# Summing exp tiles ahead of the row-sum products, and FFN1 of the last tiles by seven block products, in a fused attention and FFN kernel

## The chip, the cores and the metric

The kernel runs on one core of one Trainium2 chip. The metric is device time in microseconds (us) of one execution, lower is better, given as the median of several executions.

Engines: PE is TensorE (matrix products), PEld its weight loads, DVE is VectorE, ACT is ScalarE, POOL is GpSimd, which also issues most loads. The program lists the steps of all engines in one order, and each engine gets its instructions in that order.

## The reference

Eight batches of attention with eight heads, 576 queries, 16 beacon keys that all queries see and 576 causal keys, then an FFN with ELU over all 4,608 tokens (shortened).

```python
def _attn_ref(q, k, v, beacon_k, beacon_v):        # B, H, S, D = 8, 8, 576, 64; Nb = 16
    k_all = np.concatenate([beacon_k, k], axis=2)
    v_all = np.concatenate([beacon_v, v], axis=2)
    scores = scale * np.matmul(q, k_all.transpose(0, 1, 3, 2))
    scores = np.where(causal, -1000000000.0, scores)       # beacon keys are never masked
    scores = scores - scores.max(-1, keepdims=True)
    a = np.exp(scores)
    a /= a.sum(-1, keepdims=True) + 1e-09
    return np.matmul(a, v_all)

def _moe_ref(x, w_in, w_out):                      # x: 4608 x 512, w_in: 512 x 2048
    h = x @ w_in
    g = np.where(h > 0.0, h, np.exp(np.minimum(h, 0.0)) - 1.0)
    return g @ w_out
```

## The kernel before

The program is a list of short words, each one step: `S` scores, `x` exp (ACT), `m` causal mask (DVE), `L` row sums, `n` their reciprocals (ACT), `W` exp times values, `M` the scaling into the FFN input (DVE), `F` one row block of FFN1, `e u k` (or `e r g`) ELU (ACT and DVE), `Q` products of FFN2. FFN2 already works by seven block products from tile 2 on (a Winograd scheme: `Z` are its operand sums, `J` its copies and additions out of PSUM). `warm` and `wm` are filler: products of zeros that nobody reads. A round of the body holds the FFN1 of tile b, the FFN2 of tile b-1 and the attention of batches b and b+1. Rounds 3 to 7 have attention; what follows, with tile 8 and the last FFN2, is the tail.

```python
    def quad(b, g, qa, qe, t, half, first):          # row sums (half None) or value sums
        v16 = vt[b]
        pcs = [(j, max(a, qa), min(e, qe), c + max(a, qa) - a) for (j, a, e, c) in lays[b]
               if max(a, qa) < min(e, qe)]
        for n, (j, a, e, c) in enumerate(pcs):       # 5 key chunks, in pieces
            for i in range(4):                       # 4 heads, one 32-column group each
                h, p = 4 * g + i, 2 * g + i // 2
                nc.tensor.matmul(
                    out=t[32 * i:32 * (i + 1), a - qa:e - qa],
                    lhsT=ones[0:kc[j], :] if half is None else v16[0:kc[j], j, h, 32 * half:32 * (half + 1)],
                    rhs=ets[b, p][0:kc[j], i % 2, c:c + e - a],
                    start=(first and n == 0), stop=(n == len(pcs) - 1), skip_group_check=True)
    # ...
    def quads(b, g, half, name):
        t = psum.tile([P, 1024], FP32, tag="S", name=name)[:, 512 - QA:512 - QA + S]
        quad(b, g, 0, QA, t[:, 0:QA], half, True)    # QA = 112
        quad(b, g, QA, S, t[:, QA:S], half, True)
        return t
    # ...
    def F(t, i):                                     # FFN1: 4 products of 512 columns
        # ...
        for n_ in range(512 // w):
            fc = i * (512 // w) + n_
            for cc in range(NCC):
                nc.tensor.matmul(
                    out=h[:, n_, :], lhsT=w_in16[:, cc, P * fc:P * (fc + 1)],
                    rhs=xt[k][:, cc, a - TT * k:e - TT * k], start=(cc == 0), stop=(cc == NCC - 1))
    # ...
    def load_wi(c):                                  # c = 0..3, 512 columns each
        f_ = slice(512 * c, 512 * (c + 1))
        for g in range(2):
            for t in range(2):
                nc.gpsimd.dma_start(out=w_in16[:, 2 * g + t, f_], in_=wi_v[:, :, g, t, f_])
    # ...
    def cb(b, p):                                    # 16 beacon keys, once for each pair of heads
        qkT[b, p] = qks[p]
        nc.vector.tensor_copy(out=qkT[b, p][:, 1, 0:NB], in_=bkT[:, p, NB * b:NB * (b + 1)])
    # ...
    def r(t, i):                                     # one form of the ELU, used up to tile 2
        nc.vector.tensor_scalar(
            out=rb[t, i], in0=eb[t, i], scalar1=1.0, scalar2=1.0, op0=ALU.min, op1=ALU.subtract)
    # ...
    BODY = """
    F.b.0 e.b.0 u.b.0 k.b.0 Q.z.0.7 Z.z.1.1 S.b.1.0 x.b.1.0 m.b.1.0 S.b.1.1 x.b.1.1 m.b.1.1
    F.b.1 e.b.1 u.b.1 k.b.1 Q.z.7.14 S.b.1.2 x.b.1.2 m.b.1.2 S.b.1.3 x.b.1.3 m.b.1.3 lt.c F.b.2
    e.b.2 u.b.2 k.b.2 Q.z.14.21 J.z.0 Z.z.2.0 L.b.0 W.b.0.0 n.b.0 M.b.0.0 F.b.3 e.b.3 u.b.3
    ...
    """
```

A piece `S.b.1.0` takes two PSUM banks of a tag with two such pairs, shared by scores, row sums and value sums.

The softmax here doesn't subtract the row's maximum and nothing guards it: scores larger than these inputs give would overflow.

## Time and profile before

| | before |
|---|---|
| time, median of the first 3 runs | 352.89 us |
| span of the profiled execution | 349.8 us |
| PE busy | 335.8 us, 96%, 3,651 products |
| DVE busy | 242.3 us, 69%, 514 instructions |
| ACT busy | 281.2 us, 80% |
| POOL busy | 91.7 us, 26% |
| first FFN1 product | at 24.5 us |
| first FFN2 block product (call it Q) | at 105.7 us |
| last product ends | at 346.0 us |

From the page's slices of the kernel before, the row of DVE (busy tenths in 40 equal slices):

```profile
DVE  2672689689798758675867676767776767667661
```

DVE is at 6 to 7 tenths from the middle on: this is the room that the change wants to use.

### The profile page before, as it was taken

The page shows a single profiled execution, that of the slowest core. Times are in us where ns is not written, and L with a number is a line of the kernel's source. Part 1 is how long each engine was busy: PE and PEld are TensorE (multiplying, and loading weights), DVE is VectorE, ACT ScalarE, POOL GpSimd, SP SyncE. Part 2 cuts the span into 40 slices and gives each one's busy share as a digit, 9 for nine tenths or more (in the row PEclk, how much of TensorE's full clock was granted, in tenths as well). Part 3 has the DMA queues.
Part 4 walks back from the last instruction along what each step waited for, and adds up shares of the span by engine and source line. Part 5 has one row for each costly group of instructions (what it writes and reads, how often), then busy time and mean ns, then how long its engine had stood idle before and what let it go on. Part 6 is the DMA issues. An engine that isn't in the chain of part 4 may idle for free.

```text
span 349.8 us, 8839 instructions
## 1 busy us (share of the span) xinstructions
PE 335.8 (96%) x3651; PEld 204.6 (59%) x3651; DVE 242.3 (69%) x514; ACT 281.2 (80%) x473; POOL 91.7 (26%) x120
## 2 busy tenths in 40 slices
PE   8887998989999999999999999999999999999995
PEld 3454655444455656656665666565665666666684
DVE  2672689689798758675867676767776767667661
ACT  1893998679868997999799979997999676777731
POOL 8877446493009107300640050000000000000000
PEclk9998999999999999999999999999999999999999
DMA  9999999999709998993799359300100010010022
GB/s 117 147 150 141 185 182 174 155 140 154 136 33 152 138 114 79 175 137 73 74 172 154 66 63 182 84 2 32 62 32 2 32 60 32 30 63 30 32 90 91
DMA packets 136232, 34.67 MB, mean 99 GB/s; under 512 B 119040, under 2 KB 135680, under 8 KB 136192
## 3 DMA queue, kind: packets, MB, share of 16 engines
q0 software_dynamic: 102080, 18.51, 67.7%
q1 hardware_dynamic: 33536, 15.47, 20.1%
q8 instruction: 28, 0.46, 0.5%
q10 hardware_dynamic: 576, 0.13, 0.2%
q14 instruction: 12, 0.10, 0.1%
HBM read 37.22 MB, written 15.34 MB: 150 GB/s over the span
## 4 chain that ended last, share of the span: by engine, by line
PE 81%; ACT 5%; DMA 4%; DVE 4%; POOL 3%; issue 1%; DVEq 0%; ACTq 0%; POOLq 0%
PE hps L432 34%; PE ops L542 28%; PE ut L322 6%; PE sc L285 6%; DMA w_in<-in_moe_w_in_dram 4%; PE lt L322 3%; PE ops L478 3%; ACT et L295 2%; ACT e L442 1%; DVE qk L259 1%; POOL kst L134 1%; POOL qst L134 1%; DVE r L464 1%; ACT r L447 1%; POOL v L147 1%
## 5 line engine op out<-in xcount | busy, mean ns | idle before, releaser
L432 PE MATMUL hps<-xT,w_in 128*128 128x512 f16 (+1 forms) x640 | 148.9, 359 | 3.9 <-DMA w_in<-in_moe_w_in_dram 2.5
L457 DVE SCALAR_TENSOR_TENSOR gt<-e,r 128x512 f16<-128x512 f32 x133 | 92.0, 692 | 59.2 <-ACT r L447 54.3
L442 ACT ACTIVATE e<-hps 128x512 f32<-128x512 f32 x144 | 89.3, 621 | 33.7 <-PE hps L432 32.6
L295 ACT ACTIVATE et<-sc 128x832 f16<-128x832 f32 x128 | 106.0, 897 | 2.7 <-PE sc L285 2.6
L542 PEld LDWEIGHTS <-gt 128*128 128x128 f16 x768 | 75.1, 98 | 29.0 <-issue 0.3
L447 ACT ACTIVATE r<-hps 128x512 f16<-128x512 f32 x133 | 82.8, 624 | 5.0 <-PE hps L432 2.5
L432 PEld LDWEIGHTS <-w_in 128*128 128x128 f16 x640 | 56.5, 98 | 50.0 <-issue 7.4
L542 PE MATMUL ops<-wt,gt 128*128 128x256 f16 x384 | 52.5, 273 | 0.0
L542 PE MATMUL ops<-w_out,gt 128*128 128x256 f16 x384 | 51.4, 273 | 0.0
L311 DVE TENSOR_TENSOR et<-et,triu 128x256 f16<-128x256 f16 (+2 forms) x164 | 41.8, 357 | 13.2 <-ACT et L295 11.0
L147 POOL DMA_DIRECT2D v<-in_v_dram x40 | 35.5, 977 | 5.7 <-DMA w_out<-in_moe_w_out_dram 1.7
L499 DVE TENSOR_TENSOR gt<-gt 128x1024 f16<-128x1024 f16 x48 | 32.5, 683 | 0.0
L322 PE MATMUL ut<-et,v 128*32 128x464 f16 (+4 forms) x672 | 23.6, 283 | 1.0 <-DVE qk L263 1.0
L396 DVE TENSOR_TENSOR xT<-ut,rl 128x448 f16<-128x448 f32 (+7 forms) x56 | 22.3, 452 | 2.8 <-ACT rl L364 2.3
L322 PEld LDWEIGHTS <-v 128*32 128x32 f16 (+1 forms) x800 | 17.4, 98 | 11.5 <-issue 4.8
L285 PE MATMUL sc<-qkd 64*128 64x208 bf16 (+5 forms) x320 | 21.5, 252 | 0.0
L142 POOL DMA_DIRECT2D v<-in_beacon_v_dram x8 | 4.3, 536 | 60.1 <-PE ut L322 57.2
L551 ACT COPY sm<-ops 128x512 f32<-128x512 f32 x24 | 16.0, 667 | 5.0 <-PE ops L542 5.0
L558 DVE TENSOR_TENSOR osb<-ops,sm 128x512 f32<-128x512 f32 x24 | 16.4, 683 | 4.3 <-issue 3.7
L285 PE MATMUL sc<-qk 64*128 64x208 bf16 (+10 forms) x208 | 15.4, 246 | 2.8 <-ACT et L295 2.5
L542 PE MATMUL ops<-w_out,s 128*128 128x256 f16 x128 | 17.6, 273 | 0.0
L285 PEld LDWEIGHTS <-qkd 64*128 64x128 bf16 x320 | 11.3, 94 | 10.4 <-issue 8.2
(59 smaller groups left out, 257.3 us busy)
## 6 DMA issues: line engine op xcount, KB each, us to landing
out_dram<-osb SPq DMA_DIRECT2D x36, 256.0 KB, 2.3
v<-in_v_dram POOLq DMA_DIRECT2D x24, 128.0 KB, 6.9
scr<-in_k_dram POOLq DMA_DIRECT2D x5, 576.0 KB, 17.1
scr<-in_q_dram POOLq DMA_DIRECT2D x5, 576.0 KB, 10.3
w_in<-in_moe_w_in_dram POOLq DMA_DIRECT2D x16, 128.0 KB, 6.8
w_out<-in_moe_w_out_dram POOLq DMA_DIRECT2D x4, 512.0 KB, 9.9
v<-in_v_dram POOLq DMA_DIRECT2D x8, 112.0 KB, 5.7
v<-in_v_dram POOLq DMA_DIRECT2D x8, 80.0 KB, 7.0
```

The lines of the kernel that those rows point to most:

```text
L147: nc.gpsimd.dma_start(out=vt[b][r0:r0 + n, j, :, :], in_=v[b, :, ilo[j]:ilo[j] + n, :].rearrange("h s d -> s h d"),)
L285: nc.tensor.matmul(out=s[:, h, a - c0:e - c0], lhsT=t[D * h:D * (h + 1), 1, P * j:P * (j + 1)], rhs=t[D * h:D * (h + 1), 0, NB + qa + a - ...
L295: nc.scalar.activation(out=ets[b, p][:, :, GW * g:GW * (g + 1)], in_=sc[b, p, g][:, :, 0:GW], func=AFT.Exp, bias=0.0, scale=SCALE)
L311: nc.vector.tensor_tensor(out=o, in0=o, in1=triu[0:kc[j], :, t0:t0 + e - a], op=ALU.mult)
L322: nc.tensor.matmul(out=t[32 * i:32 * (i + 1), a - qa:e - qa], lhsT=ones[0:kc[j], :] if half is None else v16[0:kc[j], j, h, 32 * half:32 * ...
L396: nc.vector.tensor_tensor(out=x_tile(k)[:, cc, tok - TT * k:to - TT * k], in0=u[:, o:o + to - tok], in1=r[:, o:o + to - tok], op=ALU.mult)
L432: nc.tensor.matmul(out=h[:, n_, :], lhsT=w_in16[:, cc, P * fc:P * (fc + 1)], rhs=xt[k][:, cc, a - TT * k:e - TT * k], start=(cc == 0), sto ...
L442: nc.scalar.activation(out=eb[t, i], in_=flat(hp[t, i]), func=AFT.Exp, bias=0.0, scale=1.0)
L447: nc.scalar.activation(out=rb[t, i], in_=flat(hp[t, i]), func=AFT.Relu, bias=0.0, scale=1.0)
L457: nc.vector.scalar_tensor_tensor(out=half(t, i), in0=eb[t, i], scalar=1.0, in1=rb[t, i], op0=ALU.subtract, op1=ALU.min)
L499: nc.vector.tensor_tensor(out=o_, in0=a_, in1=b_, op=op_)
L542: nc.tensor.matmul(out=xy[t, n_][:, qd, :], lhsT=lw[:, P * qd:P * (qd + 1)], rhs=wt_[:, c, :], start=(first and qd == 0 and c == 0), stop= ...
```

## The change

Its intent: take products away from PE, which bounds the kernel, and pay for them on DVE, which has room. For batches 3 to 7 DVE adds the masked exp tiles of key chunks 1 to 4 into chunk 0's, and the row sum needs 8 products in place of 24. FFN1 of the last two tiles uses seven block products in place of eight for 12 of its 16 row blocks. To pay for both, the lists of all engines are written anew, some ACT copies go to DVE, and `w_in` is loaded in another shape.

```diff
     def load_wi(c):
-        f_ = slice(512 * c, 512 * (c + 1))
+        f_ = slice(DF // 2 * c, DF // 2 * (c + 1))
         for g in range(2):
-            for t in range(2):
-                nc.gpsimd.dma_start(out=w_in16[:, 2 * g + t, f_], in_=wi_v[:, :, g, t, f_])
+            for i in range(4):
+                nc.gpsimd.dma_start(
+                    out=w_in16[32 * i:32 * (i + 1), 2 * g:2 * g + 2, f_], in_=wi_v[i, :, g, :, f_])
     # ... cut: buffers; the q/k stages become fixed tiles, lent to the tail tiles later
     def cb(b, p):
         qkT[b, p] = qks[p]
-        nc.vector.tensor_copy(out=qkT[b, p][:, 1, 0:NB], in_=bkT[:, p, NB * b:NB * (b + 1)])
+        src = bkT[:, p, NB * b:NB * (b + 1)]
+        nc.vector.tensor_tensor(out=qkT[b, p][:, 1, 0:NB], in0=src, in1=src, op=ALU.max)
     # ... cut
+    def D_(b, p, n, eng="v"):
+        r_ = presum[b, p] = qks[p % 2].bitcast(FP16)[:, :, 0:S]
+        t = ets[b, p]
+        a, e, col = next((a, e, col) for (j, a, e, col) in lays[b] if j == n + 1)
+        rows = kc[n + 1]
+        o = r_[0:rows, :, a:e]
+        (nc.vector if eng == "v" else nc.gpsimd).tensor_tensor(
+            out=o, in0=t[0:rows, :, a:e] if n == 0 else o, in1=t[0:rows, :, col:col + e - a], op=ALU.add)
     # ... cut
     def quads(b, g, half, name):
         t = psum.tile([P, 1024], FP32, tag="S", name=name)[:, 512 - QA:512 - QA + S]
+        if half is None and b >= BD:
+            for a, e in ((0, QA), (QA, S)):
+                for i in range(4):
+                    k = b, 2 * g + i // 2
+                    nc.tensor.matmul(
+                        out=t[32 * i:32 * (i + 1), a:e], lhsT=ones,
+                        rhs=(presum if a else ets)[k][:, i % 2, a:e],
+                        start=True, stop=True, skip_group_check=True)
+            return t
     # ... cut
     def r(t, i):
-        nc.vector.tensor_scalar(
-            out=rb[t, i], in0=eb[t, i], scalar1=1.0, scalar2=1.0, op0=ALU.min, op1=ALU.subtract)
+        nc.vector.scalar_tensor_tensor(
+            out=rb[t, i], in0=eb[t, i], scalar=1.0, in1=one32.to_broadcast([P, 512]),
+            op0=ALU.min, op1=ALU.subtract)
     # ... cut
+    PF = [(0, (0, 0), (0, 0), True), (1, (0, 1), (1, 0), True), (0, S2, 2, False), (1, S1, 1, True),
+          (0, (1, 0), 3, False), (1, S4, (1, 1), False), (0, (1, 1), 4, False)]
+    def P_(t, g, ph):                      # a phase: 4 products of 256 columns
+        # ... cut
+    def K_(t, g, ph, eng="s"):             # its copy (ACT) or addition (DVE) out of PSUM
+        # ... cut
     # ... cut: H (sums of w_in blocks), X (sums of input blocks), E U V (ELU of a block)
     # ... cut: the whole start is listed anew, with narrow filler products wm
     BODY = """
-    F.b.0 e.b.0 u.b.0 k.b.0 Q.z.0.7 Z.z.1.1 S.b.1.0 x.b.1.0 m.b.1.0 S.b.1.1 x.b.1.1 m.b.1.1
+    S.b.1.0 S.b.1.3 F.b.0 x.b.1.3 x.b.1.0 u.b.0 lv.c m.b.1.0 F.b.1 u.b.1 e.b.0 S.b.1.2 x.b.1.2
     # ... cut
+    F.b.8 e.b.8 k.b.7 L.b.0 u.b.8 n.b.0 W.b.0.0 F.b.10 u.b.10 k.b.6 Q.z.49.56 F.b.9 k.b.8
+    S.c.0.0 S.c.0.3 e.b.10 x.c.0.0 M.b.0.0 m.b.3.0 m.b.3.1 m.b.3.2 D.b.3.0 F.b.13 D.b.3.1 k.b.10
     # ... cut
+    TAIL = """
+    P.b.0.0 P.b.0.1 Q.z.0.7 K.b.0.0 P.b.0.2 K.b.0.2 Q.z.7.14 K.b.0.1 P.b.0.3 Z.z.1.1 U.b.0.1.v
     # ... cut
+        words = (BODY3 if b == 3 else BODY if b < 8 else TAIL).split()
+        for n_, j in zip((4, 2, 1), (14, 9, 2)):
+            if b in (3, 4, 5):
+                words.insert(words.index(f"F.b.{j}") + 1, f"H.{n_}.{b - 3}")
+        if b == 7:
+            words += ["X.c.1", "X.c.3", "X.c.2", "X.c.4"]
```

## The prediction

> **What bounds the kernel now.** I read the page's slices first, to find where TensorE (PE) is not full, then the sums of stretches, then the timelines of the steady part.
>
> ```profile
> PE   8887998989999999999999999999999999999995
> ACT  1893998679868997999799979997999676777731
> PEclk9998999999999999999999999999999999999999
> DMA  9999999999709998993799359300100010010022
> ```
>
> PE is full from about slice 11 on; the clock is full too. In the first ten slices PE has gaps and the DMA engines are full: the start is a different stage. The table of stretches (length, then busy time of PE, PEld, DVE, ACT, POOL) says it in numbers:
>
> ```profile
> 20.00:35.00 15.00, 11.47 (x230) 7.47 (x227) 6.90 (x15) 8.89 (x15) 11.03 (x16) 0.89 1.29 142
> ...
> 167.42:202.98 35.56, 35.56 (x393) 21.65 (x396) 25.21 (x55) 32.92 (x57) 9.88 (x12) 1.00 1.14 115
> ...
> 285.00:315.00 30.00, 30.00 (x203) 19.71 (x202) 19.96 (x31) 22.21 (x42) 0.00 (x0) 1.00 0.11 36
> ```
>
> Each round of the body is 35.55 us with PE at 100%, ACT at 93%, DVE at 71%. After the attention ends (285 on) PE is still at 100% and the others have room. "Busy" may hide stalls, so I sum PE's work by start-to-start times from its timeline:
>
> ```profile
> 181.24 0.93 PE L542 MATMUL ops<-w_out,gt 128*128 128x256 f16 x7
> 182.10 0.90 PE L322 MATMUL lt<-et,ones 128*32 128x112 f16 x24
> 182.84 0.89 PE L322 MATMUL ut<-et,v 128*32 128x112 f16 x24
> 183.67 1.04 PE L432 MATMUL hps<-xT,w_in 128*128 128x512 f16 x4
> 184.54 0.93 PE L542 MATMUL ops<-w_out,gt 128*128 128x256 f16 x7
> 185.31 1.03 PE L432 MATMUL hps<-xT,w_in 128*128 128x512 f16 x4
> ```
>
> Here 4 FFN1 products of 512 columns take 0.87 us (0.216 each), 7 products of 256 columns 0.76 (0.109 each), 24 row-sum products in four column groups 0.74. The 7 products ahead of the row sums take 0.86, so a change of array shape costs 0.10. With these costs, the products of one round (64 FFN1, 112 FFN2, 16 scores, 2 row sums, 4 value sums, 22 changes of shape) add up to 35.6 us, against 35.55 measured. From the first FFN2 block product at 105.7 us to the last product at 346.0 the list adds up to 240.3: the trace has 240.3. So from 105.7 on nothing but PE's work counts. Ahead of that the list has 87.8 us, 6.7 of them filler, in 105.7.
>
> **What the Trainium skill says.**
> - "TensorE: Matmul & The Clock Gate", Back-to-back issue gap: N/2.4 + 2.5 ns when warm, 216 ns for 512. The trace agrees (0.216 and 0.109).
> - "TensorEngine Tiling (Array Packing)", Key Properties: a change of tiling mode drains TensorE. The trace agrees, at about 0.10 us each.
> - "SBUF — State Buffer", Who interferes with whom: a DVE copy or tensor_scalar in a 2-port mode and a GpSimd instruction exclude each other, and whoever comes second blocks fully. The trace agrees: a 16-element copy took 3.57 us while GpSimd issued loads, and a tensor_scalar that else takes 0.43 took 2.32:
>
> ```profile
> 52.48 1.36 DVE L263 COPY qk<-tp 128x1152 bf16<-128x1152 bf16 x1
> ...
> 54.29 3.57 DVE L259 COPY qk<-bkT 128x16 bf16<-128x16 bf16 x1
> ...
> 73.39 2.32 DVE L464 TENSOR_SCALAR r<-e 128x512 f16<-128x512 f32 x1 [0.73 <-ACT e L442]
> ```
>
> - "VectorE: DVE Perf Modes", The perf-mode tier table: a 16-bit tensor_tensor in SBUF runs at 2 elements a cycle, with any PSUM operand at 1. The trace agrees: 1024 f16 elements step at 0.60 us, 512 out of PSUM also at 0.60.
>
> **The change, part by part.**
>
> *Row sums.* For batches 3 to 7 the exp tiles of key chunks 1 to 4 are added into chunk 0 by DVE, and a row sum is two pieces of 112 and 464 columns in place of 1,664. Cost on PE: 0.74 x 576/1664 = 0.26, so 0.48 saved; 10 row sums, 4.8 us. DVE pays 16 additions a batch, of 928, 672, 416 and 160 f16 elements. From the 1024-element step of 0.60 and the 256-element masks (6 in 1.22 us, 0.20 each) they should step at 0.55, 0.42, 0.29 and 0.15: 1.4 us a pair of heads, 5.6 a batch. All of it beside PE.
>
> *FFN1 of the last two tiles.* 12 row blocks of 4 products of 512 columns (12 x 0.866 = 10.4 us) become 3 groups x 7 phases x 4 products of 256 columns (84 x 0.109 = 9.2): 1.2 us a tile, 2.4 in all. Added a tile: 9 copies on ACT (0.47 each, 4.2 us), 9 additions on DVE (0.60, 5.4 us), and four operand sums. DVE in tile 8: 9 additions, 16 ELU combinations at 0.61, 8 operand sums and 3 output sums at 0.60, 2 relus and 4 input sums: about 24 us, where PE needs 24.9. The weight sums (24 short DVE operations) are spread over earlier rounds.
>
> *Moved.* Three of the seven output copies of a round go from ACT to DVE: ACT -1.4 us, DVE +1.8. DVE then holds 25.2 + 5.6 + 1.8 + about 1 for weight sums = 33.6 us busy (by steps, without overlapping ends, 31.7) where PE needs about 34.6; ACT about 31.
>
> *Order.* The instruction lists have 198 changes of array shape before and 203 after: +0.5 us.
>
> *Start.* Small copies and the tensor_scalar become two-input or scalar-tensor-tensor forms that avoid the 2-port mode: at 54.3 and 73.4 DVE lost some 5 us, of which PE paid 0.6 + 1.0 + 1.0 = 2.6 in gaps. w_in comes in two halves of 1,024 columns with rows of twice the length, and the first four FFN1 blocks all need only the first half. Before, PE waited 2.5 us for w_in, and the next 80 products ran 1.7 us over their sum at a lowered clock (0.89).
>
> *Sum.* PE's list without filler goes from 321.4 to 314.7 us: -4.8 - 2.4 + 0.5 = -6.7. For the start: before, the first FFN1 product came at 24.5 us with 311.4 of work behind it, and 10.1 us were lost after it. In the changed list 303.0 lie behind it; 1.0 more lies ahead, so I set it at 25.5. Of the 10.1 I take 5 to remain (chosen: the 2.6 and about half of the 4.2 at w_in saved). Then 1.5 us of new PE stalls in the rounds and 1.5 in the tail tiles (chosen, since DVE has under 10% and under 5% of slack there). End after the last product: 3.8, as before. Span: 25.5 + 303.0 + 5 + 3 + 3.8 = 340.3. The median time was 3.1 over the profiled span (352.89 against 349.8): **343.4 us**, 2.7% less.
>
> **The rivals.**
> 1. *DVE becomes the bound.* It goes from 71% to over 90% of a round, and its additions end just ahead of the row sums that need them. For: the second pair's additions stand a few FFN1 blocks ahead of the row sum; the two summed buffers alternate, so additions wait for the row sum before. Against: by steps DVE has 3 us of slack a round. If additions ran at 1 element a cycle instead of 2 (9.6 us a batch) DVE would need more than PE and the rounds would stay at 35.5: 4.8 us given back, 348.
> 2. *The block products in the tail stall.* A phase is 0.44 us of PE, its copy or addition 0.6, and two banks alternate through 7 phases. If each group waits 1 us, 6 us are lost and the 2.4 become a loss: about 347. Against: FFN2 products stand between phases.
> 3. *The start decides.* If loads, not the order, set it, nothing is saved: 348 with the stalls, 345.5 without. If the reordered start loses only 2 us and there are no stalls, about 337.
>
> **Range and chances.** 2% is 7.06 us, so the line is 345.8. PE's list alone gives 346.1; whatever the start saves must outdo the stalls. Saving at the start has two visible sources of 2.6 and 4.2, stalls have two suspects. I take 338 to 348.5. Faster 0.75, same 0.24, slower 0.01.
>
> **What would show it.** Right: rounds of 34.6 us at PE 100%; row sums of 8 products at 0.26; additions of 928 elements stepping near 0.55; tail tiles of 24.9 and 24.0 us (26.0 and 25.2 by sum before); no DVE copy of 16 elements over 0.5 us; no PE wait for w_in over 1 us. Wrong: rounds still at 35.5 with row sums waiting for the additions; tail tiles over 26 with PE waiting for the copies out of its banks; a first FFN1 product later than 27 us; additions of 928 elements near 1 us.

## More of the kernel before

The next view is PE's waits between 20 and 60 us (engine, line, released by: us in total, times, longest). L432 is FFN1, L322 the row and value sums, L285 the scores.

```profile
PE hps L432 <- DMA w_in<-in_moe_w_in_dram: 2.5, 2, 1.3
PE sc L285 <- ACT et L295: 1.6, 4, 0.7
PE ut L322 <- DVE qk L263: 1.0, 1, 1.0
...
```

The start waits for loads, for ACT and for DVE in turn: no single cause. After Q the same view of the kernel before has no line at all.

## The result, and the profile after

| | before | after |
|---|---|---|
| time, median (lowest to highest), 4 runs each | 352.73 us (351.28 to 353.09) | 341.18 us (340.75 to 343.05) |
| span of the profiled execution | 349.8 | 339.0 |
| PE busy | 335.8, 96% | 328.4, 97% |
| DVE busy | 242.3, 69%, 514 instructions | 285.9, 84%, 662 instructions |
| ACT busy | 281.2, 80% | 280.2, 83% |
| first FFN1 product | 24.5 | 24.3 |
| first FFN2 block product (Q) | 105.7 | 98.9 |
| last product ends | 346.0 | 335.25 |

The ratio is 0.969 with a 95% interval of 0.9645 to 0.9735: faster. A ratio here is always the mean time of one kernel's fast runs over the mean of the other's fast runs of the same rounds, so it is not quite the ratio of the medians.

The slices of the changed kernel, in the same form as those of before:

```profile
PE   8988999999999999999999999999999999999995
DVE  3664998678989899889978997899799999999961
DMA  9999999999679909996799449521100111011122
```

PE's gaps at slices 7 and 9 are gone and the one at slice 4 is smaller, and DVE now stands at 8 to 9 in the rounds and 9 in the tail. The stretches of the changed kernel (length, then busy time and instruction count of PE, PEld, DVE, ACT, POOL, then the granted clock, the DMA share and GB/s): three of the start, then two rounds between like points, then tile 8.

```profile
20.00:35.00 15.00, 13.03 (x286) 8.84 (x284) 9.06 (x25) 12.74 (x20) 12.11 (x19) 1.00 1.18 172
35.00:60.00 25.00, 24.91 (x397) 16.70 (x394) 22.64 (x50) 24.17 (x37) 13.56 (x13) 1.00 1.71 186
60.00:90.00 30.00, 29.93 (x269) 13.58 (x268) 23.91 (x57) 27.82 (x48) 9.73 (x14) 1.00 1.86 157
...
126.83:162.22 35.39, 35.01 (x354) 20.91 (x354) 32.18 (x81) 31.14 (x54) 9.93 (x12) 1.00 1.15 115
...
232.60:267.44 34.84, 34.05 (x338) 20.61 (x338) 31.12 (x76) 28.71 (x51) 0.00 (x0) 1.00 0.10 32
275.00:299.60 24.60, 24.60 (x211) 20.39 (x209) 24.16 (x44) 22.42 (x43) 0.00 (x0) 1.00 0.12 38
```

From 35 us on PE is full, where before it was at 22.45 of 25. The clock between 20 and 35 is 1.00, where it was 0.89. A round takes 35.39 us, hardly less than the 35.55 of before, though the sum of its products, by the start-to-start times of the prediction, fell from 35.59 to 34.62. So 0.77 us a round is lost, of which the busy time shows only half (35.39 against 35.01). PE's timeline of a round (start, length, engine and line, tiles, array, shape, count, and in brackets the idle time just before and what ended it) has both the gain and the loss:

```profile
148.39 0.23 PE L374 MATMUL lt<-et,ones 128*32 128x112 f16 x4
148.45 0.37 PE L374 MATMUL lt<-qk,ones 128*32 128x464 f16 x4
148.69 0.89 PE L344 MATMUL ut<-et,v 128*32 128x112 f16 x24
...
152.11 0.35 PE L302 MATMUL sc<-qst 64*128 64x416 bf16 x2
152.71 0.35 PE L302 MATMUL sc<-qst 64*128 64x128 bf16 x6 [0.25 <-DVE xT L441]
```

The row sum now takes 0.30 us (148.39 to 148.69) where 24 products took 0.74. But at 152.1 the second piece of scores waits for its bank, and the bank comes free when DVE has scaled a value sum (L441). From 152.11 to 152.71 are 0.60 us, where these two products side by side need about 0.18 (the change of array shape lies before them): some 0.42 are lost, of which the bracket has only 0.25. DVE's timeline of the same round says why it was late (L360 are the new additions, L441 the scaling):

```profile
144.37 0.63 DVE L360 TENSOR_TENSOR qk<-et 128x928 f16<-128x928 f16 x1
144.92 0.68 DVE L604 TENSOR_TENSOR osb<-ops,sm 128x512 f32<-128x512 f32 x1
...
151.84 0.81 DVE L441 TENSOR_TENSOR xT<-ut,rl 128x256 f16<-128x256 f32 x2
```

The addition of 928 elements steps at 0.55 us, as predicted. The scaling that frees the bank starts at 151.84 and stands in DVE's list behind weight sums and ELU combinations, so its place in the list, not its length, holds PE; e9 below tests that. The rest of the round's 0.77 has no bracket at all. The ten score products at 145.00 take 0.70 us up to the next start, where 0.46 is usual: 0.24 are lost, and 0.11 more ahead of the FFN1 products at 147.44. Both times the FFN1 product starts 0.04 us after ACT has ended an exponential of the ELU, which reads an FFN1 bank. For the first, ACT's timeline has this one, which ends at 145.65; the FFN1 product starts at 145.70:

```profile
144.81 0.84 ACT L487 ACTIVATE e<-hps 128x512 f32<-128x512 f32 x1
```

The account of the trace, with the products' sum before and after Q:

| | before | after | difference |
|---|---|---|---|
| sum of products up to Q | 87.8 | 89.5 | +1.7 |
| sum from Q to the last product | 240.3 | 231.15 | -9.1 |
| lost ahead of Q | 17.9 | 9.4 | -8.5 |
| lost from Q on | 0 | 5.2 | +5.2 |
| last product ends | 346.0 | 335.25 | -10.7 |

The products gave 7.4 (the predicted 6.7 and 0.7 less filler), the start gave 8.5, and the rounds and the tail took 5.2 back. The 5.2 consist of 0.77 in each of rounds 3, 4 and 5, 0.37 in round 6, 1.30 in round 7, 0.82 at the first input sum of tile 8, and some 0.4 that are not placed. PE's waits between 20 and 60 us are now:

```profile
PE ub L344 <- issue: 1.0, 1, 1.0
PE hps L477 <- DMA w_in<-in_moe_w_in_dram: 0.3, 1, 0.3
...
```

The wait for w_in went from 2.5 to 0.3, and the one for DVE's qk is gone.

### The profile page after: what moved, and what is told of

It reads as the page before. It is cut to its first block, busy times and chain, and to the rows that moved or that the text cites.

```text
span 339.0 us, 8914 instructions
## 1 busy us (share of the span) xinstructions
PE 328.4 (97%) x3605; PEld 209.5 (62%) x3605; DVE 285.9 (84%) x662; ACT 280.2 (83%) x474; POOL 86.8 (26%) x120
## 4 chain that ended last, share of the span: by engine, by line
PE 56%; ACT 19%; DVE 10%; issue 7%; DMA 4%; POOL 3%; POOLq 0%; DVEq 0%
PE ops L588 19%; PE hps L477 17%; ACT et L312 10%; PE hps L660 5%; PE ut L344 5%; ACT e L487 4%; ACT r L492 4%; PE sc L302 4%; DVE gt L502 3%; PE ops L524 3%; DMA kst<-in_k_dram 2%; DMA w_in<-in_moe_w_in_dram 2%; DVE xT L441 1%; PE lt L344 1%; POOL qst L136 1%
## 5 line engine op out<-in xcount | busy, mean ns | idle before, releaser
L312 ACT ACTIVATE et<-sc 128x832 f16<-128x832 f32 x128 | 112.2, 944 | 24.4 <-PE sc L302 23.9
L477 PE MATMUL hps<-xT,w_in 128*128 128x512 f16 (+1 forms) x544 | 119.2, 355 | 1.3 <-DMA w_in<-in_moe_w_in_dram 0.3
L502 DVE SCALAR_TENSOR_TENSOR gt<-e,r 128x512 f16<-128x512 f32 x108 | 72.2, 683 | 15.0 <-ACT e L487 9.3
L487 ACT ACTIVATE e<-hps 128x512 f32<-128x512 f32 x120 | 79.3, 685 | 1.9 <-PE hps L477 1.9
L477 PEld LDWEIGHTS <-w_in 128*128 128x128 f16 x544 | 49.1, 98 | 44.8 <-issue 5.6
L492 ACT ACTIVATE r<-hps 128x512 f16<-128x512 f32 x108 | 71.3, 682 | 1.6 <-PE hps L477 0.9
L329 DVE TENSOR_TENSOR et<-et,triu 128x256 f16<-128x256 f16 (+2 forms) x164 | 35.9, 266 | 10.4 <-ACT et L312 10.3
L441 DVE TENSOR_TENSOR xT<-ut,rl 128x448 f16<-128x448 f32 (+7 forms) x56 | 22.5, 446 | 1.0 <-ACT rl L409 0.6
L360 DVE TENSOR_TENSOR qk<-qk,et 128x672 f16<-128x672 f16 (+2 forms) x60 | 22.0, 367 | 0.6
L670 ACT COPY kst<-hps 128x512 f32<-128x512 f32 x18 | 10.6, 589 | 8.8 <-PE hps L660 8.3
L524 PE MATMUL ops<-w_out,gt 128*128 128x512 f16 x64 | 16.3, 380 | 0.0
L699 DVE SCALAR_TENSOR_TENSOR gt<-e,r 128x512 f16<-128x512 f32 x24 | 15.8, 685 | 0.4 <-ACT e L682 0.2
```

The source lines that it names most:

```text
L312: nc.scalar.activation(out=ets[b, p][:, :, GW * g:GW * (g + 1)], in_=sc[b, p, g][:, :, 0:GW], func=AFT.Exp, bias=0.0, scale=SCALE)
L329: nc.vector.tensor_tensor(out=o, in0=o, in1=triu[0:kc[j], :, t0:t0 + e - a], op=ALU.mult)
L441: nc.vector.tensor_tensor(out=x_tile(k)[:, cc, tok - TT * k:to - TT * k], in0=u[:, o:o + to - tok], in1=r[:, o:o + to - tok], op=ALU.mult)
L477: nc.tensor.matmul(out=h[:, n_, :], lhsT=w_in16[:, cc, P * fc:P * (fc + 1)], rhs=xt[k][:, cc, a - TT * k:e - TT * k], start=(cc == 0), sto ...
L487: nc.scalar.activation(out=eb[t, i], in_=flat(hp[t, i]), func=AFT.Exp, bias=0.0, scale=1.0)
L492: nc.scalar.activation(out=rb[t, i], in_=flat(hp[t, i]), func=AFT.Relu, bias=0.0, scale=1.0)
```

## The experiments

Twelve kernels were run, all correct, each timed beside the kernel before on the same chip. "Q" is the first FFN2 block product of the profiled execution, "Q to end" the time from it to the last product.

| kernel | time, median | ratio to before, 95% | Q at | Q to end | a round |
|---|---|---|---|---|---|
| before | 352.7 | | 105.7 | 240.3 | 35.55 |
| after | 341.18 | 0.969 (0.9645 to 0.9735) | 98.9 | 236.4 | 35.39 |
| e6_old_start | 352.04 | 0.9998 (0.9964 to 1.0032) | 108.9 | 236.5 | 35.39 |
| e5_old_w_in | 345.96 | 0.9811 (0.9778 to 0.9844) | 104.7 | 236.35 | 35.39 |
| e4_two_port | 341.73 | 0.9697 (0.9661 to 0.9733) | 100.75 | 236.4 | 35.40 |
| e1_no_presum | 342.93 | 0.9746 (0.9697 to 0.9795) | 101.2 | 238.5 | 35.86 |
| e3_before_presum | 365.49 | 1.0376 (1.0324 to 1.0428) | 104.2 | 253.8 | 37.68 |
| e2_plain_ffn1 | 343.38 | 0.9743 (0.9707 to 0.9779) | 98.2 | 238.1 | 34.99 |
| e2b_plain_old_tail | 340.87 | 0.9669 (0.9633 to 0.9705) | 99.4 | 236.0 | 34.98 |
| e7_early_x | 340.19 | 0.9652 (0.9625 to 0.9678) | 98.4 | 236.45 | 35.39 |
| e8_h_shift | 341.11 | 0.9674 (0.9642 to 0.9706) | 99.5 | 236.4 | 35.39 |
| e9_round_order | 339.59 | 0.9609 (0.9577 to 0.9641) | 100.9 | 235.3 | 34.88 |
| e10_all | 341.02 | 0.966 (0.9631 to 0.9689) | 99.0 | 235.9 | 34.88 |
| e11_rounds_last | 338.43 | 0.9594 (0.9574 to 0.9614) | 98.2 | 234.3 | 34.88 |

One warning first: eight of the kernels in this table (after, e2, e2b, e7 to e11) have the same start, and Q of their profiled executions lies between 98.2 and 100.9. The same code varies by 2.7 us there, a good part of it in one wait near 31 us that no record explains ("issue": 2.1 us in e9, 1.0 in the changed kernel, absent in e2, e8 and e11). "Q to end" does not have this noise (236.4 in after, e4, e5 and e8 alike), and small effects after Q are read from it.

### e6_old_start: the changed rounds and tail behind the start of before

```diff
-    lq.0.0.0.4 warm.12 lq.0.1.0.4 ident bt bk cb.0.3 cb.0.0 T.0.1.0 cb.0.1 wm.9 ...
+    lq.0.0.0.4 warm.12 ident bt bk cb.0.0 lq.0.1.0.4 warm.8 cb.0.1 cb.0.2 T.0.1.0 ...
+    (the start list of before; load_wi, cb and r as before; the additions of batch 3 at its end)
```

> The changed kernel with the start of the kernel before: its order of steps up to batch 3, its w_in loads, its copies and tensor_scalar; rounds and tail as changed. Theory (the start saved 8.5 us of waits: 17.9 us lost ahead of the first FFN2 block product before, 9.4 after): first block product near 107 us in place of 98.9, time 349 to 350. Rival (the start is set by the loads, and the gain lies in the rounds): 342 to 344.

It took 352.04 us: the ratio to before is 0.9998, and nothing of the change's gain is left. PE's waits between 20 and 60 us have the old lines back, the largest being:

```profile
PE hps L475 <- DMA w_in<-in_moe_w_in_dram: 2.9, 3, 1.7
...
```

So the new start is worth 10.9 us in time (352.04 against 341.18), and 10.0 in the trace up to Q (108.9 against 98.9). Some of that is the seam: the old start is not fitted to the new rounds and waits 0.9 us there, twice for DVE. After Q, e6 is as long as the changed kernel (236.5 against 236.4), which shows that the start's gain is not given back later. The two mathematical parts of the change take 7.2 us of products away, yet behind the old start they are worth some 0.5 us of span: from Q to the end e6 is 3.7 shorter than before, but its Q comes 3.2 later, with 1.8 us more of products listed ahead of it and the 0.9 of the seam.

### e5_old_w_in: w_in in 16 loads of 128 partitions and 512 columns again

```diff
-        f_ = slice(DF // 2 * c, DF // 2 * (c + 1))
-        for g in range(2):
-            for i in range(4):
-                nc.gpsimd.dma_start(
-                    out=w_in16[32 * i:32 * (i + 1), 2 * g:2 * g + 2, f_], in_=wi_v[i, :, g, :, f_])
+        for h_ in (2 * c, 2 * c + 1):
+            f_ = slice(512 * h_, 512 * (h_ + 1))
+            for g in range(2):
+                for t in range(2):
+                    nc.gpsimd.dma_start(out=w_in16[:, 2 * g + t, f_], in_=wi_v[:, :, g, t, f_])
```

> The changed kernel with w_in loaded as before: 16 loads of 128 partitions x 512 columns in place of 32 partitions x 2 x 1024, in the same places of the GpSimd order. Theory (rows of twice the length make the weights land sooner): waits for w_in of 2 us or more come back behind the first FFN1 product and the value sums after them run at a lowered clock: 343 to 345. Rival (the order of the first FFN1 blocks, all of which need the first half only, is what counts): 341 to 342.

345.96 us against 341.18: the shape of the loads alone is worth 4.8 us. The theory was half right. PE does not wait for w_in in it; PE's waits between 20 and 60 us name the loads queued behind w_in, the q and k of batch 1 (L266 is their transpose):

```profile
PE tp L266 <- DMA qst<-in_q_dram: 3.2, 1, 3.2
PE tp L266 <- DMA kst<-in_k_dram: 0.7, 1, 0.7
...
```

Behind these waits the lowered clock did come: between 35 and 45 us the granted clock is 0.68, where the changed kernel has 1.00, and eight FFN1 products of 256 columns at 41.82 take 1.82 us up to the next start, where eight like them at 33.17 took 0.98. So the 4.8 us are waits and slow products together.

The transfers between 15 and 45 us tell why the loads land late. The line is that of the DMA view; first before, then the changed kernel, then e5:

```profile
DMA packets 14864, 4.83 MB, mean 161 GB/s; under 512 B 10130, under 2 KB 14860, under 8 KB 14860
```

```profile
DMA packets 7142, 5.62 MB, mean 187 GB/s; under 512 B 2247, under 2 KB 6113, under 8 KB 7137
```

```profile
DMA packets 13147, 4.72 MB, mean 157 GB/s; under 512 B 8277, under 2 KB 13142, under 8 KB 13142
```

The engines are full in all three. With half the packets they move 0.9 MB more in the same 30 us than in e5, and 0.9 MB at 187 GB/s is 4.8 us. That this equals the difference in time is an estimate that fits, not a proof. The Trainium skill, "DMA: Bandwidth & Descriptors", Why small descriptors are slow, names a fixed cost for each packet; this trace agrees in kind. POOL spends 0.68 us on one such load in the old shape and 0.55 in the new one.

### e4_two_port: the DVE copies and tensor_scalars of before, in the new order

```diff
-        src = bkT[:, p, NB * b:NB * (b + 1)]
-        nc.vector.tensor_tensor(out=qkT[b, p][:, 1, 0:NB], in0=src, in1=src, op=ALU.max)
+        nc.vector.tensor_copy(out=qkT[b, p][:, 1, 0:NB], in_=bkT[:, p, NB * b:NB * (b + 1)])
...
-        nc.vector.scalar_tensor_tensor(
-            out=rb[t, i], in0=eb[t, i], scalar=1.0, in1=one32.to_broadcast([P, 512]),
-            op0=ALU.min, op1=ALU.subtract)
+        nc.vector.tensor_scalar(
+            out=rb[t, i], in0=eb[t, i], scalar1=1.0, scalar2=1.0, op0=ALU.min, op1=ALU.subtract)
```

> The changed kernel with the DVE copies of 16 elements and the tensor_scalar as they were before (forms that exclude GpSimd). The old start with the new rounds took 352.0 us, so the start is worth some 10 us; which part of it? Theory (DVE shut out by GpSimd cost 3 of the 10 us): 342.5 to 344.5, with at least one DVE copy of 16 elements or a tensor_scalar of over 1.5 us and a TensorE wait behind it. Rival (the new order of steps is what counts; GpSimd issues its loads elsewhere): 341 to 342, no such wait.

341.73 us, ratio 0.9697 against the 0.969 of the changed kernel: no difference that the runs can show. By their intervals one of up to about 2 us could hide, so the theory's 3 us is out, though not the lower end of its range, and the rival has the time right. Its "no such wait" is not: DVE is still shut out by GpSimd at times (the lock, below), as DVE's timeline of e4 shows:

```profile
48.38 1.42 DVE L508 TENSOR_SCALAR r<-e 128x512 f16<-128x512 f32 x1
...
50.44 2.21 DVE L275 COPY hi<-bkT 128x16 bf16<-128x16 bf16 x1
50.51 2.41 DVE L508 TENSOR_SCALAR r<-e 128x512 f16<-128x512 f32 x1
```

These three are long; of the other instructions of the two forms the tensor_scalars take about 0.42 us and the copies 0.16 to 0.66. But most of what DVE loses there lies beside other work: PE waits once for DVE, 0.94 us at 53.7. The scalar-tensor-tensor form of the changed kernel takes 0.68 us each of the twelve times, 8.2 us in all, and the twelve tensor_scalars of e4 take 8.1, the long ones included. So the new form buys freedom from the lock at about the price that the lock takes.

Of the 10 us that the start is worth, load shape explains about 5 and the instruction forms about none. The remainder, about 5, is left to the new order, found by subtraction alone: e6 and e5 differ by 6.1 us in time and 4.2 in Q, and both figures include the seam's 0.9. It was not taken apart further, and whether the DVE forms would matter in the old order was not run.

### e1_no_presum: the changed kernel with row sums of 24 products and without the additions

```diff
-        if half is None and b >= BD:
+        if half is None and b >= B:          # never
...
-    k.b.4 D.b.1.0 J.z.1 Q.z.35.42 D.b.1.1 D.b.1.2 F.b.6 e.b.5 ...
+    k.b.4 J.z.1 Q.z.35.42 F.b.6 e.b.5 ...    (all D words out)
```

> The changed kernel with the row sums as before (24 products each, no DVE additions), all else kept. Theory (rounds are bound by TensorE's list): 10 row sums x 0.48 = +4.8 us of products; DVE gets 5.6 us a round back, so the 0.4 to 0.8 us a round that TensorE now loses beyond its list go: rounds of 35.6 to 35.8 us, time 341.2 + 3 to 5 = 344 to 346 us. Rival (DVE is already co-bound, and the additions give back most of what they save): rounds stay near 35.4 and the time rises by 1 us or less, to 342.

342.93 us, 1.75 more than the changed kernel. The intervals of the two overlap, so the trace must decide. In it the rounds are 35.86 against 35.39, and from Q to end 238.5 against 236.4: the row sums give 2.1 us where their products gave 4.8. Without the additions a round loses 0.27 over its sum, with them 0.77. So in this order of steps the additions do cost PE time, 0.5 us a round, though all of them fit beside its work. In the order of e9, below, a round with the additions loses only 0.26: the cost is that of the order.

### e3_before_presum: the kernel before with the additions alone

```diff
-    F.b.1 e.b.1 ... x.b.1.2 m.b.1.2 S.b.1.3 x.b.1.3 m.b.1.3 lt.c F.b.2
+    F.b.1 e.b.1 ... x.b.1.2 m.b.1.2 D.b.1.0 S.b.1.3 x.b.1.3 m.b.1.3 D.b.1.1 D.b.1.2 D.b.1.3 lt.c F.b.2
     (likewise behind the masks of pairs 2, 3 and 0; the short row sum; D_ as in the change)
```

> The kernel before with the DVE additions and the short row sums alone, in its own order of steps, each pair's additions placed right after its masks. Theory: the list of the rounds falls by 4.85 us and 0 to 2 us of it comes back as waits of the row sum for the additions: 348 to 350 us against 352.7. Rival (the additions need the new order of steps to pay): row sums wait for DVE by 1 us or more each, and the time is 351 to 353.

365.49 us, 13 more than before and far outside of what either theory expected. Each round has two waits of PE like these (PE's timeline, L352 the row sum, L338 the additions):

```profile
168.76 0.37 PE L352 MATMUL lt<-qk,ones 128*32 128x464 f16 x2 [1.04 <-DVE qk L338]
...
189.48 0.37 PE L352 MATMUL lt<-qk,ones 128*32 128x464 f16 x2 [1.32 <-DVE qk L338]
```

They account for 7.1 us from 180 on. Rounds grew from 35.55 to 37.68 with DVE at a load that it has room for. The additions put right behind the masks come due at once with the row sums, and delay what stands behind them. The same instructions in the order of the changed kernel gain 2.1. The list of products says what may be gained; whether it is gained depends on the place of each addition.

### e8_h_shift: the sums of w_in blocks in rounds 4 to 6 in place of 3 to 5

```diff
-                if b in (3, 4, 5):
-                    words.insert(words.index(f"F.b.{j}") + 1, f"H.{n_}.{b - 3}")
+                if b in (4, 5, 6):
+                    words.insert(words.index(f"F.b.{j}") + 1, f"H.{n_}.{b - 4}")
```

> The changed kernel with the weight sums (12 short DVE operations a round with their steps) in the rounds of batches 4 to 6 in place of 3 to 5. Theory (DVE's filling sets what a round loses beyond TensorE's list): the period that ends in batch 6 goes from 35.0 to 35.4 us, the first round of batch 3 shortens by 0.4, total time the same within 0.3 us: 341.2. Rival (the rounds differ for another reason, such as GpSimd's loads that end with batch 6): periods stay 35.4, 35.4, 35.0.

The total did not move (341.11), and it was not meant to. The rounds moved as the theory said: the stretch ahead of the first full round fell from 33.20 to 32.80, and round 6 rose from 34.99 to 35.39. Six short DVE sums (81 DVE instructions in such a round against 75; the expectation's twelve was a miscount) cost PE 0.4 us in whichever round they stand, in this order of steps.

### e9_round_order: two moves against the waits for banks

The scaling that frees the bank goes ahead of an ELU combination, and the first two score pieces of the next round go ahead of the last FFN2 products of this one.

```diff
+        if b < 8:
+            words.remove("M.b.0.0")
+            words.insert(words.index("k.b.8"), "M.b.0.0")
+            if b > 3:
+                words.remove("S.b.1.0")
+                words.remove("S.b.1.3")
+            i = words.index("Q.z.105.112")
+            words[i:i] = ["S.c.1.0", "S.c.1.3"]
```

> The changed kernel with two moves in each round: the first scaling of a round goes ahead of an ELU combination on DVE (it frees the bank that the second score product of the next batch waits for), and the first two score products of the next round go ahead of the last 7 FFN2 products of this one (ACT, idle 3.8 us there, starts its exponentials 0.76 us sooner, so the later score product finds its bank free). Theory (a round loses 0.77 us beyond its list at these two waits, 0.33 and 0.36): periods of batches 4 to 6 of 34.7 to 34.9 us in place of 35.4, 35.4, 35.0; time -1.2 to -2.5, 338.7 to 340. Rival (DVE or ACT is full over the round and the wait only moves): periods within 0.2 of before, time 341.

Rounds fell from 35.39 to 34.88 with the same instructions, the wait at the scores is gone, and the time is 339.59. So two thirds of the 0.77 were order, 0.42 of it the wait for the scaling. Rounds with the weight sums and without them now take the same 34.88, so in this order these sums cost PE nothing. Round 7, though, got longer (35.28 for 34.84), with a new wait in PE's waits of e9:

```profile
PE lt L374 <- DVE qk L360: 1.0, 1, 1.0
...
```

### e10_all: e9, with the input sums of tile 8 earlier and round 7's FFN2 copies on ACT

```diff
-                words += ["X.c.1", "X.c.3", "X.c.2", "X.c.4"]
+                i = words.index("M.b.1.0") + 1
+                words[i:i] = ["X.c.1", "X.c.2", "X.c.3", "X.c.4"]
+                words = [x_[:-2] if x_.startswith("J.z") and x_.endswith(".v") else x_ for x_ in words]
```

> As the run before it, with the early input sums for tile 8 and, in the last attention round, the three output copies put back on ACT, which is idle for a fifth of that round. Theory: the waits of that round (0.4 for ACT or the bank, 0.6 for the additions) fall by half or more, and the 0.8 us at the input sums go: another -0.8 to -1.5, time 337.3 to 339. Rival: the additions of that round still come late and only the 0.6 to 1.0 us of the early input sums is seen.

The theory failed. 341.02 us is slower than e9: the 0.8 at the input sums did go, but the last round took 36.27 us, the wait of 1.0 for the additions stayed, and PE's wait for ACT's exponential of the ELU rose from 0.2 to 0.7. ACT has free time in round 7 (28.71 of 34.84 us busy in the changed kernel), but it seems not when these copies are due. The run makes two changes at once, and which of them costs how much was not separated.

### e11_rounds_last: e9 without its move in round 7, and one weight sum behind the additions there

```diff
         if b < 8:
-            words.remove("M.b.0.0")
-            words.insert(words.index("k.b.8"), "M.b.0.0")
+            if b < 7:
+                words.remove("M.b.0.0")
+                words.insert(words.index("k.b.8"), "M.b.0.0")
...
         if b == 7:
+            words.remove("H.3.2")
+            words.insert(words.index("D.b.2.3") + 1, "H.3.2")
```

> The two moves in the rounds as in the run with them alone (periods 34.9 in place of 35.4, 35.4, 35.0), but in the last attention round DVE keeps the changed kernel's order, except that two short weight sums go behind the last addition, for which the row sum waits. In the run with the two moves alone that round grew from 34.8 to 35.3 us, as the row sum there waited 1.0 us for the additions in place of 0.45. Theory (that round is bound by DVE up to the row sum): the wait is 0.1 or less, the round 34.3 to 34.6, first FFN2 block product to last product 234.2 to 234.8 us in place of 236.4, time 338.5 to 339.8. Rival (another wait takes its place): the round stays at 34.8 and the stretch at 235 or more.

As expected: round 7 takes 34.30, the wait at the row sum is gone, and from Q to end are 234.3 against 236.4. The time is 338.43 us, ratio 0.9594 (0.9574 to 0.9614), the best of all; its interval lies below that of the changed kernel. Here are PE's waits from 180 us on, first of the changed kernel, then of e11:

```profile
PE hps L660 <- DVE qst L643: 0.8, 1, 0.8
PE lt L374 <- DVE qk L360: 0.4, 1, 0.4
PE sc L302 <- DVE xT L441: 0.3, 1, 0.3
...
```

```profile
PE hps L660 <- DVE qst L643: 0.8, 1, 0.8
PE hps L477 <- ACT e L487: 0.2, 1, 0.2
```

### e2_plain_ffn1 and e2b_plain_old_tail: FFN1 of the last two tiles by plain products

The first lists the two tiles in the rounds' new order, the second in the order of the kernel before.

```diff
-        words = (BODY3 if b == 3 else BODY if b < 8 else TAIL).split()
+        words = (BODY3 if b == 3 else BODY).split()                          # e2
+        words = (BODY3 if b == 3 else BODY if b < 8 else OLD).split()        # e2b, OLD = BODY of before
-        if SGB == 0:             (the H and X words)
+        if False:
```

> The changed kernel with FFN1 of the last two tiles by plain products (64 of 512 columns each), in the rounds' order of steps; no weight sums, no input sums, no copies out of the FFN1 banks. Theory (the block products save 2.4 us of the list and cost about as much): the 0.8 us wait ahead of the first block product goes, and the rounds of batches 3 to 5 lose the 1.2 us of weight sums and shorten from 35.4 to about 35.0: net +0.1 to +0.8, 341.3 to 342. Rival (their cost is all hidden): +2.4, 343.6.

> Plain FFN1 for the last two tiles as in the first run of that kind, whose own tail lost 1.2 us by its order, now in the order of steps of the kernel before, which ran these tiles with no wait. Theory (the block products save 2.4 us of list and cost 0.8 at the input sums, 0.4 a round in three rounds for the weight sums and about 0.3 in the last round): 341.0 to 341.9, within 0.7 us of the changed kernel. Rival (the earlier 343.4 was not its order): 343 or more.

e2 took 343.38 us, 2.2 more than the changed kernel, and alone would have praised the block products. But its tail has new waits of its own, 0.6 for ACT's relu and 0.6 for a DVE copy, since the rounds' order without attention is a poor one. e2b, with the order of before and no such wait, took 340.87 and 236.0 from Q to end, against 341.18 and 236.4. In the order of the changed kernel, the block products of FFN1 gain nothing. The 2.4 us of products are there, and they are paid back: 0.4 a round in three rounds for the weight sums (a round without them takes 34.98), 0.8 for the input sums at tile 8, and about 0.4 in round 7. In the order of e9 and e11 the first of these prices is not paid; whether the block products gain there was not run.

### e7_early_x: the four input sums of tile 8 right behind the scaling that they need

```diff
-                words += ["X.c.1", "X.c.3", "X.c.2", "X.c.4"]
+                i = words.index("M.b.1.0") + 1
+                words[i:i] = ["X.c.1", "X.c.2", "X.c.3", "X.c.4"]
```

> The changed kernel with the four input sums for tile 8 moved on DVE from the end of the last attention round to right behind the product that completes the input. Theory: the wait of 0.8 us ahead of the first S2 product of tile 8 goes, and nothing else moves: span and time -0.5 to -0.8, 340.4 to 340.7. Rival (DVE is full there, so the sums only push the ELU combinations back): no gain, 341.2.

The wait of 0.8 is gone, and from Q to end are 236.45 us, as before: two waits of 0.3 and 0.2 us for other DVE steps stand in its place, and the rest is lost without a record. DVE is full at that point (24.16 of 24.60 us), so what is moved forward moves something else back. The time of 340.19 is 1.0 less than that of the changed kernel; the trace puts this at the start, which varies by more.

## Why the prediction was right or wrong

The total was right: 343.4 predicted, 341.18 measured, 338 to 348.5 as the range, and "faster" at 0.75. It was right in part by luck, with errors of opposite sign: the start came out better than set and the rounds worse. The terms of its sum beside the trace:

| term | predicted | measured |
|---|---|---|
| first FFN1 product | 25.5 | 24.3 |
| products behind it | 303.0 | 303 |
| lost between it and Q | 5 | 2.7 |
| lost in rounds and tail | 3 | 5.2 |
| after the last product | 3.8 | 3.75 |
| median time minus span | 3.1 | 2.2 |

**The products.** Right: the work behind the first FFN1 product is 303 us. The 216 ns that it took from the Trainium skill is that page's figure for a product alone; the page's own figure for a stream is lower and would have been wrong here (see the last section). A row sum takes 0.30 us where 0.26 was said; the additions step at the 0.55 said for 928 elements, and the rival with one element a cycle is out.

**The start.** Wrong in its size and in its reasons. The step that failed is "Of the 10.1 I take 5 to remain (chosen: the 2.6 and about half of the 4.2 at w_in saved)". 2.7 remained in the profiled execution (1.3 to 4.8 in the eight kernels with this start), and the first FFN1 product came 1.2 earlier than set (24.2 to 26.3 in the eight). The 2.6 for the DVE forms is not what they bring in the new order: e4 undoes them, and the runs show no difference beyond some 2 us of noise. The w_in shape is worth 4.8 (e5), more than the half of 4.2, and it does not work through PE's wait for w_in but through all loads queued behind it, and through the slow products that follow the wait. The third part, the order, the prediction did not price at all, and it is about 5 by subtraction. Rival 3's last sentence, 337 for a start that loses 2 and no stalls, had the start right.

**The rounds.** The step "1.5 us of new PE stalls in the rounds" was mis-sized: it was 4.4. The text's "Against: by steps DVE has 3 us of slack a round" was true as a sum, and the rounds have just that (32.18 busy of 35.39). It is not an argument against stalls: e9 and e11 take half a microsecond a round away with the same instructions, e8 moves 0.4 a round with 1.2 us of short sums. The stalls came mostly from banks freed late by DVE and ACT, and only in round 7 from additions that end behind their row sum, which was rival 1's picture. So the predicted rounds of 34.6 at PE 100% are wrong: 35.39 at 99%, and the busy share hides half of the loss. Of 4.8 us by the row sums 2.1 arrived (e1).

**The tail tiles.** Right in the trace: after the 0.8 us at the first input sum, PE runs through both tiles at the sum of its products, and rival 2's stalls between phases did not come. What was missed is that their price is paid elsewhere, in rounds 3 to 5 and 7, by the weight sums that were "spread over earlier rounds". With that, FFN1's 2.4 us are gone (e2b).

**The offset.** The 3.1 set a median against the span of one execution. That execution itself took 351.5 us, 1.7 over its span, and the changed kernel's median lies 2.2 over its own. Two small sums in the text are off as well: 352.89 less 6.7 is 346.2, not 346.1, and rival 2's 6 us in place of the 1.5 set for the tail give 348, not 347.

Open: what in the new start order brings the 5 us; what the "issue" wait near 31 us is; what the output copies moved from ACT to DVE bring alone, which no run took apart; and how the 0.8 us at tile 8 could be had with DVE full.

## What to carry to other kernels

Sum PE's products by start-to-start times and hold the sum against the period: where they agree, only fewer products help, and where they differ, the difference is the price of a list order, though the engine shows busy. Work moved to an engine with room is not free, because it delays what stands behind it in that queue: trace each late release of a bank to its place in the list before counting the gain. In a start that is full of loads, count packets and what stands in the queue behind a load, not only the wait for the load itself.

## What the Trainium skill lacked or had wrong

- "TensorE: Matmul & The Clock Gate", Back-to-back issue gap, puts a stream of weight loads and products at about 131 ns for 512 columns and says that 216 ns over-counts. Here every product has its own weight load (3,651 of each before), and 512 columns step at 0.216 us: the sum with that figure is 240.3 us from Q on before, and the trace has 240.3.
- "Perfetto Trace Analysis", Identifying the Most-Contended Engine, rightly distrusts the share of time with a matmul, and offers that of weight loads, beside the share of peak FLOPs. In a round of before the weight loads are 21.65 of 35.55 us (61%) with no headroom at all. The start-to-start sum is what showed both the full PE before and the 0.77 us a round lost after.
- "TensorEngine Tiling (Array Packing)", Key Properties, gives no size for the drain at a change of tiling: about 0.10 us here.
- "DMA: Bandwidth & Descriptors" has no figure for converting loads issued by GpSimd in the two shapes used here. At full engines 13,147 packets moved 157 GB/s (e5) and 7,142 moved 187 (after); the two kernels differ by 4.8 us.
- "SBUF — State Buffer", Who interferes with whom, says who blocks, and e4 agrees (a copy of 16 elements took 2.21 us where 0.16 is usual). It gives no time for escaping the lock: here the form that avoids it takes 0.68 us where the tensor_scalar takes 0.42 undisturbed and 2.41 at worst.
